# Sliding-window attention and a gated convolution FFN on one core: a written-out order of all instructions replaced by another

## The chip, the cores and the metric

The kernel runs on one NeuronCore of one Trainium2 chip. The time is the device time of one launch in microseconds (us). Engines are named as in the profile: PE (TensorE: matmuls), PEld (its weight loads), DVE (VectorE), ACT (ScalarE), POOL (GpSimd) and SP (SyncE, which here only issues transfers). Each engine carries out its own instructions strictly in the order in which they stand in its program; an instruction that waits holds up everything behind it on that engine.

## The reference

```python
batch, n_heads, seq, head_dim = (8, 8, 576, 64)
...
    scores = scale * np.matmul(q, k.transpose(0, 1, 3, 2))   # scale = 1 / sqrt(64)
    mask = np.abs(pos[:, None] - pos[None, :]) <= 32
    scores = np.where(mask, scores, -1000000000.0)
    attn = softmax(scores)
    x = np.matmul(attn, v)          # heads side by side: (8, 576, 512)
...
    h = np.maximum(x @ w_in, 0.0)   # w_in: 512 x 1024
    for k in range(3):
        conv_out += conv_w[k][None, None, :] * hp[:, k:k + S, :]   # along the sequence, per channel
    gate = 1.0 / (1.0 + np.exp(-conv_out))
    return (h * gate @ w_out)       # w_out: 1024 x 512
```

All inputs and the output are float32.

## The kernel before

**Tiling.** Attention is done in 36 units of two 64-row query tiles each (units 4 and 6 are cut into two halves, a and b); a tile needs 128 keys. The FFN is done in 12 chunks of 384 rows, three chunks to two batches. Products run in bf16 into eight PSUM banks.

**Operations.** `build` lists some 1,200 named operations with the slots that they read and write. The names, which the plan below uses too, are: LQK (load a q or k tile; in `LQKb.yz` b is the batch, y is 0 for q and 1 for k, z the half or 01 pair of heads), CQK (cast it to bf16), TR (transpose it on PE: 18 matmuls), EV (copy the transpose out of PSUM), LV, CV, VO (load v, cast it, copy it shifted by half a tile), LWI, CWI, LWO, CWO (load and cast the two weights), SC (scores), EX (exp, ACT), MA (mask, DVE), AV (attention times v, 16 matmuls), NO (normalize, two DVE instructions), XT and XE (transpose of the result on PE, and its copy out) or, from unit 20 on, XD (the same by a transposing transfer), PH and RE (first FFN product and relu), RO (rotation of h by 32, 64 or 96 partitions, two transfers on SP or two copies on DVE), CO (convolution: 48 small matmuls on diagonal weights), TA (tanh, ACT), GA (gate, DVE), YY (second FFN product: 8 matmuls), YC (copy out of PSUM), YS (store). MK and DG make masks and diagonals. F512 is a matmul of zeros whose result nobody reads.

**What sets the order.** There is no scheduler at build time: `PLAN` is a text of words, carried out from the first to the last (lines 761 to 776). A word is an operation, `/A`, `/D` or `/S` names the engine of a copy or rotation (ACT, DVE, SP), and the digits behind `@` name its PSUM banks. So the text sets the order on every engine and who does each copy. The numbers in `build` (an engine's cost, `size` for a transfer) are not used when the kernel is built; they belong to the search that wrote the text.

**Queues.** All loads, stores, rotations and transposing transfers are issued by SP in the order of the text, except half of each first-batch q or k load, which ACT issues (line 449). q, k and the two weights pass through six staging tiles `st0` to `st5`, so a load waits for the cast of what was there before; v passes through `vst`, with five places. The first-batch loads use st0 to st3; w_in's pieces 1, 2, 3 and 0 use st4, st5, st0 and st1; the four tiles of batch 1 use st2, st3, st4 and st5.

**Lines.** Loads of q and k L450 (batches 0 and 1) and L453, v L461, w_in L475, w_out L487 and L489, store L738, rotation L688 and L689, transposing transfer L651. Copies and casts are L380 on ACT and L382 on DVE; exp L544, mask L615, normalize L634 and L635, relu L682, tanh L715, gate L722; matmuls L390, transposes L393.

Of the kernel before, what the change touches and what calls it, by code (L numbers as in the profile page):

```python
# [72 lines left out]
def build(k, ud=UD):  # L73
# [22 lines left out]
    def load_qk(b, parts):  # L96
        early = b < HB
        for z in parts:
            for y in range(2):
                s, q = nxt("st", NST), nxt("qkb", NQB)  # L100
                add(f"LQK{b}.{y}{z}", {"SP": 1.27 if early else 0.52}, lambda e, a=(b, y, z, s): k.load_qk(*a),
                    w=[("st", s)], size=1.95, desc=256, cnt=2 if early else 1)
                add(f"CQK{b}.{y}{z}", {"DVE": 0.67, "ACT": 1.02},
                    lambda e, a=(s, q): k.cast_qk(e, *a), r=[("st", s)], w=[("qkb", q)], port=1)
                ps = [Slot(), Slot()]
                add(f"TR{b}.{y}{z}", {"PE": 0.27}, lambda e, a=(q, ps): k.turn(*a), r=[("qkb", q)], w=ps, alloc=ps, mode="r64")
                for x in range(2):
                    add(f"EV{b}.{y}{z}{x}", {"ACT": 0.53, "DVE": 0.67}, lambda e, a=(b, y, z, x, ps[x]): k.evac_qk(e, *a),
                        r=[ps[x]], w=[("qkT", b % 2, y, z, x)], uses=[ps[x]])
# [139 lines left out]
F512@0 F512@0 F512@0 F512@0 F512@0 F512@0 F512@0 F512@0 F512@0 F512@0 F512@0 AV0@57 MA1 SC4b@24 NO0.0 EX4b.1 EX4b.0
VO0.11 CWI3/A VO0.02 NO0.1 F512@0 F512@0 AV1@25 MA4b SC5@41 NO1.0 CV0.3/A VO0.13 CWI1/A NO1.1 VO0.12 EX5.1 VO0.03  # L250
LQK1.01 CWI2/D F512@0 F512@0 F512@0 F512@0 AV2@52 XT1@7 NO2.0 AV3@16 XE1/A XT0@3 LQK1.11 NO3.1 SC6a@50 XE0/A NO2.1
AV4a@76 EX5.0 NO3.0 PH0.5a@3 LV1.3 EX6a.1 XT2@4 EX6a.0 NO4a.1 XT3@1 LV1.1 XE2/A CWI0/D LV1.2 RE0.5a XE3/A CV1.0/D
F512@2 F512@2 PH0.1a@3 MA6a LV1.4 CQK1.01/A AV4b@46 NO4a.0 PH0.0a@1 NO4b.0 PH0.7b@5 XT4a@7 NO4b.1 RE0.7b PH0.0b@0
RE0.0a PH0.6b@4 XE4a/D TR1.01@16 CQK1.11/D PH0.7a@7 EV1.010/A EV1.011/D TR1.11@52 LQK2.10 RE0.6b RE0.7a PH1.4a@1
LWO0 EV1.111/D EV1.110/A PH1.0a@7 RE0.0b PH0.4a@6 RE1.0a SC7@25 RE1.4a CV1.1/D RE0.4a SC8@70 CV1.3/D EX7.0 PH0.6a@1
MA5 SC6b@64 EX8.0 PH0.2a@2 CV1.2/D EX6b.0 PH1.3a@7 RE0.1a EX7.1 VO1.00 PH0.5b@6 PH0.3a@3 EX6b.1 CV1.4/D XT4b@5
RE0.2a RE1.3a PH0.4b@4 RE0.6a VO1.10 PH0.1b@2 RE0.5b EX8.1 RO0.3 PH0.2b@1 MA7 PH0.3b@6 RE0.2b AV5@70 XE4b/A MA6b
LQK2.00 RE0.3a NO5.1 RE0.3b AV6a@15 CQK2.10/A NO5.0 RO0.1 AV6b@36 PH1.5a@0 NO6a.1 XT5@7 RE0.4b NO6a.0 RE1.5a LWO3
PH1.6a@5 NO6b.0 RE1.6a XT6a@1 RE0.1b AV7@04 MA8 XE5/A LWO2 PH1.2a@3 XE6a/A NO7.1 PH1.1a@2 AV8@75 NO6b.1 RE1.1a LWO1
PH1.5b@4 RE1.2a NO8.1 CO0.0@2136 RE1.5b NO8.0 XT6b@4 NO7.0 TA0.03 PH1.2b@5 TA0.00 PH1.7b@7 XE6b/D RE1.2b PH1.3b@0  # L260
GA0.03 TA0.01 PH1.6b@4 RE1.3b PH1.4b@5 RE1.7b GA0.01 TA0.02 RO1.1 XT8@0 XT7@7 GA0.00 RE1.4b PH1.7a@1 RE1.6b XE8/D
XE7/A CO0.1@6524 RO1.2/D CWO3/A PH2.5@7 RO0.2/D TA0.11 PH2.7@0 RE1.7a TA0.13 GA0.11 RO1.3 TA0.12 PH2.6@1 GA0.02
TA0.10 GA0.13 PH2.2@5 RE2.6 CWO0/D RE2.7 TR2.10@43 GA0.12 RE2.2 PH1.0b@1 LQK2.01 GA0.10 PH2.4@0 RE1.0b LV2.3 RE2.5
CWO1/D PH1.1b@1 CO1.0@6257 CWO2/D RE1.1b LQK2.11 EV2.101/D LV2.1 YY0.1@1 TA1.02 EV2.100/D LV2.4 TA1.03 TA1.01 LV2.2
GA1.02 RE2.4 GA1.01 TA1.00 CO1.1@0543 YC0.1/A CQK2.01/D YY0.2@2 TA1.10 GA1.03 TA1.11 GA1.00 CQK2.00/A LV2.0 GA1.10
LQK3.00 GA1.11 TR2.01@67 TA1.12 LQK3.10 TR2.00@01 RO2.2/D EV2.011/A YY0.0@5 LQK3.11 EV2.000/A CQK2.11/D RO2.3 TA1.13
YC0.2/D EV2.001/A TR2.11@07 EV2.010/A GA1.13 PH2.3@1 EV2.110/D EV2.111/A LQK3.01 YC0.0/A PH2.1@6 GA1.12 CV2.4/A
CV2.1/D SC12@07 CV2.3/D SC10@45 EX12.1 YY1.1@3 CV2.2/D LV3.3 EX10.1 VO2.10 RE2.1 CV2.0/D EX10.0 VO2.00 EX12.0 SC9@65
SC11@47 MA10 EX9.0 YY1.2@2 EX9.1 MA12 EX11.1 CQK3.00/D RE2.3 EX11.0 MA9 AV10@75 RO2.1 AV12@16 NO10.0 YY1.0@4
CQK3.10/A NO10.1 LV3.1 MA11 YC1.2/A YC1.1/A NO12.1 AV9@25 LV3.4 CQK3.11/A NO12.0 TR3.00@70 AV11@63 NO9.1 XT12@1 YS0  # L270
EV3.001/A NO11.1 PH2.0@5 YC1.0/A NO9.0 XE12/A XT10@3 TR3.10@40 NO11.0 LV3.2 EV3.000/A XT9@2 XE10/D XT11@6 RE2.0
EV3.101/D CQK3.01/A LV3.0 CO2.0@5371 XE9/D XE11/D TR3.11@20 EV3.100/D TA2.02 PH3.1@6 YS1 TA2.03 GA2.02 TA2.01
LQK4.11 PH3.4@4 GA2.03 RE3.1 LQK4.00 EV3.110/A GA2.01 PH3.0@7 EV3.111/D RE3.4 CO2.1@3162 TA2.00 RE3.0 GA2.00
TR3.01@04 TA2.10 PH3.5@7 TA2.13 GA2.10 TA2.11 PH3.2@5 EV3.011/D EV3.010/A PH3.6@3 TA2.12 GA2.13 RE3.5 GA2.12 PH3.3@4
RE3.2 GA2.11 CV3.3/A SC14@72 RO3.2/D SC13@56 EX14.1 YY2.0@1 EX13.0 CV3.1/D CV3.4/D EX14.0 CV3.2/D EX13.1 MA14
SC15@75 RE3.3 SC16@62 MA13 EX15.0 YY2.1@0 RO3.1 CV3.0/D EX16.0 VO3.10 EX15.1 LV4.2 VO3.00 YC2.0/A LQK4.10 AV13@56
EX16.1 MA15 PH3.7@1 YC2.1/A NO13.0 RE3.6 SC17@27 NO13.1 RE3.7 AV15@50 EX17.1 MA16 RO3.3 CO3.0@3416 EX17.0 NO15.1
# [532 lines left out]
```

## Time and profile before

| | us |
|---|---|
| median of 3 runs (lowest, highest) | 230.08 (228.53, 230.11) |
| the profiled execution, device time | 229.58 |
| its span, first to last instruction | 227.9 |
| PE, DVE, ACT busy in the span | 203.4, 190.1, 180.2 |

The device time of the profiled execution is 1.68 us more than its span. A busy PE is not PE at its peak: matmuls are pipelined and the profile models their ends. In rows of groups stand the busy time, the mean duration of one in ns and the idle time just before them; a timeline's row gives start, length, engine, line, tiles and, in brackets, the idle time before it and what ended it.

### The profile page before, as it was taken

The page shows a single profiled execution, that of the slowest core. Times are in us where ns is not written, and L with a number is a line of the kernel's source. Part 1 is how long each engine was busy: PE and PEld are TensorE (multiplying, and loading weights), DVE is VectorE, ACT ScalarE, POOL GpSimd, SP SyncE. Part 2 cuts the span into 40 slices and gives each one's busy share as a digit, 9 for nine tenths or more (in the row PEclk, how much of TensorE's full clock was granted, in tenths as well). Part 3 has the DMA queues.
Part 4 walks back from the last instruction along what each step waited for, and adds up shares of the span by engine and source line. Part 5 has one row for each costly group of instructions (what it writes and reads, how often), then busy time and mean ns, then how long its engine had stood idle before and what let it go on. Part 6 is the DMA issues. An engine that isn't in the chain of part 4 may idle for free.

```text
span 227.9 us, 8845 instructions
## 1 busy us (share of the span) xinstructions
PE 203.4 (89%) x3711; PEld 121.1 (53%) x3741; DVE 190.1 (83%) x459; ACT 180.2 (79%) x393; POOL 1.2 (1%) x8
## 2 busy tenths in 40 slices
PE   0279789999999999999999999999999979999990
PEld 0174468776445655655556556554655545545450
DVE  7568999999999999999988999879999599574830
ACT  2278688979999999789899998999849876649710
POOL 2000000000000000000000000000000000000000
PEclk9999999999999999999999999999999999999998
DMA  6999699697999996997996795999977854523253
GB/s 196 308 263 278 197 258 248 170 265 181 304 269 325 283 291 199 230 280 219 370 209 124 236 327 117 128 322 148 391 143 174 203 181 89 176 76 141 74 187 102
DMA packets 67187, 49.45 MB, mean 217 GB/s; under 512 B 48044, under 2 KB 53444, under 8 KB 67140
## 3 DMA queue, kind: packets, MB, share of 16 engines
q1 hardware_dynamic: 66528, 47.62, 78.9%
q10 hardware_dynamic: 612, 1.19, 1.6%
q8 instruction: 31, 0.51, 1.0%
q14 instruction: 16, 0.13, 0.2%
HBM read 32.52 MB, written 9.44 MB: 184 GB/s over the span
## 4 chain that ended last, share of the span: by engine, by line
PE 44%; DVE 24%; DMA 11%; ACT 9%; issue 5%; SPq 4%; DVEq 0%; ACTq 0%
PE ps L390 41%; DMA vst<-in_v_dram 6%; DVE gT L722 5%; DVE xn L635 5%; PE ps L393 3%; DMA st<-in_q_dram 3%; ACT hh L682 3%; DVE attn L615 3%; ACT attn L544 2%; DVE vo L382 2%; DVE qkb L382 2%; ACT ps L715 2%; DVE rec L634 2%; DMA hh<-hh 2%; SPq L461 2%
## 5 line engine op out<-in xcount | busy, mean ns | idle before, releaser
L390 PE MATMUL ps<-xT,w_in_sb 128*128 128x385 bf16 (+3 forms) x448 | 72.3, 305 | 1.1 <-DVE w_in_sb L382 0.3
L390 PE MATMUL ps<-w_out_sb,gT 128*128 128x512 bf16 (+1 forms) x269 | 65.0, 373 | 1.8 <-issue 0.5
L682 ACT ACTIVATE hh<-ps 128x385 bf16<-128x385 f32 (+3 forms) x112 | 48.0, 476 | 10.2 <-PE ps L390 9.8
L722 DVE SCALAR_TENSOR_TENSOR gT<-ps,hh 128x384 bf16<-128x384 f32 x96 | 48.7, 550 | 7.4 <-ACT ps L715 6.4
L390 PEld LDWEIGHTS <-w_in_sb 128*128 128x128 bf16 x448 | 39.4, 98 | 24.0 <-issue 3.3
L715 ACT ACTIVATE ps<-ps 128x384 f32<-128x384 f32 x96 | 42.1, 497 | 6.6 <-PE ps L390 6.1
L544 ACT ACTIVATE attn<-ps 128x512 bf16<-128x512 f32 (+1 forms) x76 | 40.6, 615 | 6.0 <-PE ps L390 4.3
L390 PEld LDWEIGHTS <-gT 128*128 128x128 bf16 x296 | 27.1, 97 | 29.1 <-issue 1.3
L635 DVE TENSOR_TENSOR xn<-ps,rec 128x256 bf16<-128x256 f32 (+1 forms) x76 | 32.2, 424 | 2.6
L380 ACT COPY qkT<-ps 128x576 bf16<-128x576 bf16 x42 | 26.4, 672 | 4.7 <-PE ps L393 4.7
L615 DVE TENSOR_TENSOR attn<-attn,masks 128x1024 bf16<-128x1024 bf16 (+1 forms) x38 | 24.5, 659 | 2.5 <-ACT attn L544 2.2
L393 PE MATMUL ps<-ident,qkb 64*128 64x64 bf16 x576 | 14.3, 199 | 11.0 <-DVE qkb L382 10.4
L380 ACT COPY y<-ps 128x512 f32<-128x512 f32 (+1 forms) x27 | 16.4, 612 | 8.5 <-PE ps L390 8.5
L390 PE MATMUL ps<-hh,diag 32*32 32x384 bf16 x1152 | 20.3, 327 | 0.0
L393 PEld LDWEIGHTS <-qkb 64*128 64x128 bf16 x576 | 11.4, 100 | 16.4 <-DVE qkb L382 11.6
L382 DVE COPY qkT<-ps 128x576 bf16<-128x576 bf16 x22 | 16.3, 751 | 3.0 <-PE ps L393 2.8
L382 DVE CAST qkb<-st 128x1152 bf16<-128x1152 f32 x22 | 16.6, 753 | 2.1 <-DMA st<-in_q_dram 2.0
L390 PEld LDWEIGHTS <-attn 128*64 128x64 bf16 x576 | 12.6, 110 | 10.6 <-issue 5.2
L390 PE MATMUL ps<-ve,attn 128*64 128x65 bf16 x320 | 15.6, 197 | 1.4 <-DVE xn L635 1.0
L390 PEld LDWEIGHTS <-diag 32*32 32x32 bf16 x1152 | 11.8, 88 | 7.8 <-issue 4.2
L390 PEld LDWEIGHTS <-qkT 64*128 64x128 bf16 x576 | 11.1, 99 | 7.5 <-issue 6.0
L390 PE MATMUL ps<-qkT 64*128 64x64 bf16 x576 | 13.5, 196 | 1.7 <-DVE qkb L382 1.3
(57 smaller groups left out, 136.6 us busy)
## 6 DMA issues: line engine op xcount, KB each, us to landing
out_dram<-y SPq DMA_DIRECT2D x11, 768.0 KB, 6.3
st<-in_k_dram SPq DMA_DIRECT2D x12, 576.0 KB, 6.6
st<-in_q_dram SPq DMA_DIRECT2D x12, 576.0 KB, 5.7
vst<-in_v_dram SPq DMA_DIRECT2D x24, 256.0 KB, 6.4
vst<-in_v_dram SPq DMA_DIRECT2D x16, 192.0 KB, 5.9
hh<-hh SPq DMA_DIRECT2D x16, 144.8 KB, 3.0
st<-in_moe_w_in_dram SPq DMA_DIRECT2D x4, 512.0 KB, 7.2
st<-in_k_dram SPq DMA_DIRECT2D x6, 288.0 KB, 5.5
```

The source lines that it names most:

```text
L380: self.do(nc.scalar.copy(out=out, in_=in_))
L382: self.do(nc.vector.tensor_copy(out=out, in_=in_))
L390: self.do(self.nc.tensor.matmul(*a, **kw))
L393: self.do(self.nc.tensor.transpose(out=out, in_=in_, identity=ident))
L461: self.do(self.dq.dma_start(self.vst[s0 - lo:s1 - lo, c], self.v_[b, :, s0:s1, :].rearrange("h p d -> p h d")))
L544: self.do(self.nc.scalar.activation(at[:, lo:hi], self.ps(ps)[:, lo:hi], AF.Exp, bias=0.0, scale=self.scale))
L615: self.do(self.nc.vector.tensor_tensor(out=at, in0=at, in1=m, op=ALU.mult))
L634: self.do(self.nc.vector.reciprocal(rec, po[:, :, 64]))
L635: self.do(self.nc.vector.tensor_tensor(out=self.xn[x][lo:hi, 4 * g:4 * g + 4, :], in0=po[:, :, 0:64], in1=rec[:, :, None].broadcast_to([hi ...
L682: self.do(self.nc.scalar.activation(o, i_, AF.Relu, bias=0.0, scale=0.5))
L715: self.do(self.nc.scalar.activation(z, z, AF.Tanh, bias=0.0, scale=1.0))
L722: self.do(self.nc.vector.scalar_tensor_tensor(out=o, in0=z, scalar=1.0, in1=self.taps(kind, 0, 128, 6 + 2 * j + g if j else g, 1), op0=ALU ...
```

## The change

Three numbers of `build` change: what a first-batch q or k load costs SP (1.27 to 0.65) and how long it takes (`size` 1.95 to 1.65, and 2.1 for batch 1). Since these are not used in building, they change nothing by themselves. What changes the program is `PLAN`, which is replaced from its first line to its last.

```diff
-                add(f"LQK{b}.{y}{z}", {"SP": 1.27 if early else 0.52}, lambda e, a=(b, y, z, s): k.load_qk(*a),
-                    w=[("st", s)], size=1.95, desc=256, cnt=2 if early else 1)
+                add(f"LQK{b}.{y}{z}", {"SP": 0.65 if b == 0 else 1.27 if early else 0.52}, lambda e, a=(b, y, z, s): k.load_qk(*a),
+                    w=[("st", s)], size=1.65 if b == 0 else 2.1 if early else 1.95, desc=256, cnt=2 if early else 1)
...
-LQK0.11 LQK0.01 LQK0.10 LQK0.00 MK CQK0.11/D LV0.1 TR0.11@01 CQK0.01/D EV0.111/A TR0.01@23 LQK1.00 EV0.110/A
...
+LQK0.01 LQK0.10 LQK0.00 LQK0.11 MK LV0.4 CQK0.01/D CQK0.10/D TR0.01@01 LQK1.00 TR0.10@23 EV0.011/D LV0.1 CQK0.00/A
...
```

The operations are the same, but for the matmuls of zeros: 25 before, 20 now. Before, 17 of them stand ahead of the first AV, six between it and the first PH, and two between the first and the second PH. Now 7 stand ahead of the first AV, 12 between it and the first PH, and one behind that.

The engines of copies change: CQK 10 on ACT and 22 on DVE before, 11 and 21 now; EV 42 and 22, now 44 and 20; CV 15 and 25, now 13 and 27; CWO 1 and 3, now 3 and 1; XE 10 and 12, now 12 and 10 (the two that move are half-size); YC 27 and 10, now 25 and 12 (one of the two is half-size); of twelve rotations RO by 64 partitions on DVE one, of chunk 10, goes to SP. Ahead of the first CO there are seven CQK on DVE before and five now.

SP's first loads, before; `st` with its number is the staging tile, `vst` is v, 96x8x64 its first or last tile of a batch.

```order
L450 DMA st3_64<-in_k_dram 128x1x576
L450 DMA st2_63<-in_q_dram 128x1x576
L450 DMA st1_62<-in_k_dram 128x1x576
L450 DMA st0_61<-in_q_dram 128x1x576
L461 DMA vst_67<-in_v_dram 128x8x64
L450 DMA st2_63<-in_q_dram 128x1x576 x2
L450 DMA st3_64<-in_k_dram 128x1x576 x2
L461 DMA vst_67<-in_v_dram 96x8x64
L461 DMA vst_67<-in_v_dram 128x8x64
L461 DMA vst_67<-in_v_dram 96x8x64
L475 DMA st0_61<-in_moe_w_in_dram 128x4x256
L475 DMA st4_65<-in_moe_w_in_dram 128x4x256
```

The same place of SP now, from the third load of batch 0 on:

```order
L450 DMA st0_61<-in_q_dram 128x1x576
L450 DMA st3_64<-in_k_dram 128x1x576
L461 DMA vst_67<-in_v_dram 96x8x64
L450 DMA st2_63<-in_q_dram 128x1x576 x2
L461 DMA vst_67<-in_v_dram 128x8x64 x2
L461 DMA vst_67<-in_v_dram 96x8x64
L450 DMA st3_64<-in_k_dram 128x1x576 x2
L461 DMA vst_67<-in_v_dram 128x8x64
L475 DMA st4_65<-in_moe_w_in_dram 128x4x256
L475 DMA st5_66<-in_moe_w_in_dram 128x4x256
L475 DMA st1_62<-in_moe_w_in_dram 128x4x256
L461 DMA vst_67<-in_v_dram 96x8x64
```

The second tile of batch 1 (st3) now stands behind four of the five v tiles of batch 0; the last v tile comes behind it. The v tile of rows 0 to 95, LV0.0, is the last 96x8x64 row ahead of the weights before, and now the one ahead of that st3 row. The fourth piece of w_in (st0) has gone from the first place among the weights to one not shown here, behind the last two tiles of batch 1 (st4, st5).

ACT a little later, around the casts of the first weights, before (`ve0` a cast v tile, `qkT1` batch 1's transposes, `w_in_sb` the weight):

```order
L380 COPY qkT1_78<-ps7_122 128x4x144
L380 CAST ve0_73<-vst_67 128x8x64
L380 COPY qkT1_78<-ps5_120 128x4x144
L380 CAST ve0_73<-vst_67 128x8x64
L544 ACTIVATE attn0_84<-ps4_119 128x256
L544 ACTIVATE attn0_84<-ps2_117 128x256
L380 CAST w_in_sb_79<-st0_61 128x4x256
L380 CAST ve0_73<-vst_67 128x8x64
L380 CAST w_in_sb_79<-st4_65 128x4x256
```

And now:

```order
L380 CAST ve0_73<-vst_67 128x8x64
L380 CAST qkb0_68<-st3_64 128x2x9x64
L544 ACTIVATE attn2_86<-ps2_117 128x512
L380 COPY qkT1_78<-ps4_119 128x4x144
L380 COPY qkT1_78<-ps1_116 128x4x144
L380 COPY qkT1_78<-ps6_121 128x4x144
L380 CAST w_in_sb_79<-st4_65 128x4x256
L380 COPY qkT1_78<-ps0_115 128x4x144
L380 CAST w_in_sb_79<-st5_66 128x4x256
```

The cast of batch 1's second tile (`qkb0<-st3`) has come to ACT from DVE, and the cast of st5, which frees that tile for batch 1's last load, has come from DVE as well.

DVE where batch 7's v is used, before (`attn` masks, `ve1` cast v, `vo1` shifted v, `rec` and `xn` normalize):

```order
L615 TENSOR_TENSOR attn4_88<-attn4_88,masks_83 128x1024
L615 TENSOR_TENSOR attn3_87<-attn3_87,masks_83 128x1024
L382 CAST ve1_74<-vst_67 128x8x64 x3
L382 COPY vo1_76<-ve1_74 64x2080
L615 TENSOR_TENSOR attn0_84<-attn0_84,masks_83 128x1024
L382 COPY vo1_76<-ve1_74 64x2080
L634 RECIPROCAL rec_103<-ps4_119 128x4
```

And now:

```order
L615 TENSOR_TENSOR attn3_87<-attn3_87,masks_83 128x1024
L382 CAST ve1_74<-vst_67 128x8x64
L615 TENSOR_TENSOR attn4_88<-attn4_88,masks_83 128x1024
L634 RECIPROCAL rec_103<-ps2_117 128x4
L635 TENSOR_TENSOR xn1_90<-ps2_117,rec_103 128x256
L382 CAST ve1_74<-vst_67 128x8x64
L382 COPY vo1_76<-ve1_74 64x2080
L615 TENSOR_TENSOR attn0_84<-attn0_84,masks_83 128x1024
L382 COPY vo1_76<-ve1_74 64x2080
```

One of the three casts of v in a row has gone to ACT, and a normalize (two instructions) has come in ahead of the rest. On SP the four late v tiles of batch 7 stood one ahead of chunk 6's store and three behind it; now all four stand behind it. On PE one more PH (four matmuls) now stands ahead of the AV that reads the last `vo1`.

More of the change, by code (lines that the diff above doesn't have):

```diff
@@ L249 @@
[L249 to L253, printed above, removed]
```

151 lines of the change are left out of this document (78 added, 73 removed).

## The prediction

> **What bounds the kernel now.** I read the busy times first, then the span cut into stages, then the chain of waits, and the timelines where the chain points.
>
> ```profile
> PE 203.4 (89%) x3711; PEld 121.1 (53%) x3741; DVE 190.1 (83%) x459; ACT 180.2 (79%) x393; POOL 1.2 (1%) x8
> 20.00:48.00 28.00, 25.18 (x447) 17.57 (x447) 25.76 (x73) 21.31 (x54) 0.00 (x0) 1.00 0.89 232
> 48.00:90.00 42.00, 41.13 (x782) 24.30 (x786) 40.48 (x92) 40.84 (x88) 0.00 (x0) 1.00 0.98 264
> 90.00:190.00 100.00, 96.43 (x1901) 55.97 (x1918) 90.69 (x215) 88.10 (x188) 0.00 (x0) 1.00 0.87 221
> 190.00:223.00 33.00, 32.44 (x406) 16.95 (x408) 19.69 (x44) 19.83 (x47) 0.00 (x0) 1.00 0.42 130
> PE 44%; DVE 24%; DMA 11%; ACT 9%; issue 5%; SPq 4%; DVEq 0%; ACTq 0%
> ```
>
> In a stage's row stand its length, then the busy time of PE, PEld, DVE, ACT and POOL. There are four regimes. From 20 to 48 us DVE is busy 25.76 of 28 and ACT only 21.31, so DVE carries the stage and ACT has 6.7 us free. From 48 to 90 all three are full: ACT has 1.2 us free, DVE 1.5. From 90 to 190 they share the load, with 9.3 us free on DVE and 11.9 on ACT. From 190 on attention is over, DVE and ACT are idle two fifths of the time, and PE alone sets the pace. So a shorter start, or less DVE work while DVE carries, is worth its full size only if the last stage then begins earlier; and no stage has an engine with much to spare.
>
> The two places where the chain of waits runs through a transfer (start, length, what):
>
> ```profile
> 12.84 8.17 DMA vst<-in_v_dram
> 21.04 0.63 ACT ve L380
> 21.69 0.29 DVE vo L382
> ...
> 22.00 0.69 DVE attn L615
> ...
> 176.32 6.18 DMA vst<-in_v_dram
> ```
>
> At the start the last early v tile, LV0.0, is issued at 12.84 and cast at 21.04; the shifted copy and the mask of unit 0 follow, and only then AV0. At 176 the same happens to batch 7's last v tile.
>
> ```profile
> 18.92 2.32 PE L390 MATMUL ps<-zz 128*128 128x512 bf16 x5
> 21.02 2.31 PE L390 MATMUL ps<-zz 128*128 128x512 bf16 x9
> 23.48 0.22 PE L390 MATMUL ps<-ve,attn 128*64 128x65 bf16 x1
> 30.51 0.26 PE L390 MATMUL ps<-xT,w_in_sb 128*128 128x193 bf16 x1
> 48.23 0.47 ACT L715 ACTIVATE ps<-ps 128x384 f32<-128x384 f32 x1 [0.59 <-PE ps L390]
> ```
>
> PE fills the wait with matmuls of zeros; AV0 comes at 23.48, the first PH at 30.51, the first tanh, so the end of the first CO, at 48.23.
>
> **Copies that change engine.** Durations come from the groups of instructions (busy time, then mean ns of one).
>
> ```profile
> L382 DVE CAST qkb<-st 128x1152 bf16<-128x1152 f32 x22 | 16.6, 753 | 2.1 <-DMA st<-in_q_dram 2.0
> L380 ACT CAST qkb<-st 128x1152 bf16<-128x1152 f32 x10 | 12.2, 1216 | 0.0
> L382 DVE COPY qkT<-ps 128x576 bf16<-128x576 bf16 x22 | 16.3, 751 | 3.0 <-PE ps L393 2.8 <-PE ps L390 0.2
> L380 ACT COPY qkT<-ps 128x576 bf16<-128x576 bf16 x42 | 26.4, 672 | 4.7 <-PE ps L393 4.7
> L382 DVE CAST w_out_sb<-st 128x1024 bf16<-128x1024 f32 x3 | 2.0, 683 | 0.0
> L380 ACT CAST w_out_sb<-st 128x1024 bf16<-128x1024 f32 x1 | 1.1, 1088 | 0.0
> L382 DVE CAST ve<-vst 128x512 bf16<-128x512 f32 x25 | 10.2, 424 | 1.9 <-DMA vst<-in_v_dram 1.8
> L380 ACT CAST ve<-vst 128x512 bf16<-128x512 f32 x15 | 10.0, 670 | 2.1 <-DMA vst<-in_v_dram 2.1
> L382 DVE COPY y<-ps 128x512 f32<-128x512 f32 x10 | 6.9, 687 | 2.6 <-PE ps L390 2.4
> L380 ACT COPY y<-ps 128x512 f32<-128x512 f32 x25 | 15.6, 632 | 7.7 <-PE ps L390 7.7
> L382 DVE COPY xT<-ps 128x256 bf16<-128x256 bf16 x2 | 0.6, 286 | 0.0
> L380 ACT COPY xT<-ps 128x256 bf16<-128x256 bf16 x2 | 0.8, 386 | 0.0
> ```
>
> Up to CO9.1, about where the last stage begins, DVE loses two CWO, one CQK, two EV and two half-size XE and gains one YC and two CV: -1.37 - 0.75 - 1.50 - 0.57 + 0.69 + 0.85 = -2.65 us. ACT gets the reverse: +2.18 + 1.22 + 1.34 + 0.77 - 0.63 - 1.34 = +3.54.
>
> Where this lies decides what it is worth. Ahead of the first CO, DVE has two CQK and one half XE less, 1.51 + 0.29 = 1.8 us; one of these casts comes back behind it. ACT has one CQK and one CWO more there, 2.3, in a stage in which it has 6.7 free. So these 1.8 us come off the engine that carries the stage, and I take **-1.8**; at best nothing more of this, at worst 0, if DVE waits that much longer.
>
> Between the first CO and CO9.1 the rest is left: DVE -2.65 + 1.8 = -0.9, ACT +3.54 - 2.3, some +1.2. The two are near each other in free time there, so I take **0**, with -0.9 and +1.2 as ends.
>
> **The loads of the start.** LV0.0 now has batch 1's second tile (two rows of 288 KB) behind it instead of ahead.
>
> ```profile
> 10.00:20.00 10.00, 6.86 (x150) 5.28 (x152) 7.66 (x13) 7.39 (x15) 0.00 (x0) 1.00 1.04 255
> 16.84 0.76 DVE L382 COPY qkT<-ps 128x576 bf16<-128x576 bf16 x1 [1.66 <-PE ps L393]
> ```
>
> At the 255 GB/s of this stage 576 KB are 2.3 us, so LV0.0 lands at about 18.7; the mask of unit 0 (0.69) now stands ahead of the shifted copy and is done by then. AV0 comes at about 18.7 + 0.63 + 0.29, near 19.6 in place of 23.48. But then the next load is late: DVE's cast CV0.2 needs the last v tile, LV0.2, which now has the same tiles ahead of it that LV0.0 had, and one v tile of 256 KB (1.0 us) more, so it lands near 22. The two masks, normalizes and AVs behind that cast wait for it, in order. DVE's old wait of 1.66 for a transpose goes, since that copy is ACT's now; a wait of 1 to 2.5 us for LV0.2 takes its place. I count **0**. The ends are -2.4 (of AV0's lead of 3.9 the 1.5 that the new wait surely takes is gone) and +1.
>
> **The matmuls of zeros.** Five fewer. They stand where PE waits anyway, and cost nothing as long as what follows is not ready. The rows above show what they do: the first five start 0.42 us apart ((2.32 - 0.63) / 4, with 0.63 the last one's length, an estimate), the next nine 0.24, most of them 0.215. So PE runs at half its pace until about 21.3 us, 2.4 us into the row of them. Now seven stand ahead of AV0, and the twelve behind it are cut up by waits. I count 0, since the 18 transposes, AV0 and three more of them follow closely.
>
> [...]
>
> **Batch 7's v tiles.**
>
> ```profile
> 173.78 0.54 SPq L738 DMA_DIRECT2D out_dram<-y  x1
> 174.36 5.50 SPq L461 DMA_DIRECT2D vst<-in_v_dram  x3
> 182.23 0.43 DVE L382 CAST ve<-vst 128x512 bf16<-128x512 f32 x1 [0.94 <-DMA vst<-in_v_dram]
> 184.90 0.22 PE L390 MATMUL ps<-vo,attn 128*64 128x65 bf16 x1 [1.48 <-DVE vo L382]
> ```
>
> PE stands 1.48 us because the last shifted copy of v is late. Now one more PH, four matmuls or some 0.7 us of PE, stands ahead of that AV, and one cast fewer (0.42) ahead of the copy on DVE. Against it, the first of the four tiles now also goes behind chunk 6's store (768 KB). I take **-0.5**, between -1.48 and +1.
>
> **The tail.**
>
> ```profile
> 214.31 8.39 PE L390 MATMUL ps<-w_out_sb,gT 128*128 128x512 bf16 x46
> 214.48 2.42 DVE L722 SCALAR_TENSOR_TENSOR gT<-ps,hh 128x384 bf16<-128x384 f32 x5
> ```
>
> The last gate ends at 216.90; the last chunk's YY begins after the two YY of chunk 10, two fifths of this run (16 of 40 full matmuls' worth), at 217.7. So there is 0.8 us to spare. Now the last chunk's two PH for the rotation by 96 partitions are followed by one other PH and not three, so its rotation starts nearer to the end by two PH, some 1.4 us, which the spare time covers in part. I take **+0.3**, between 0 and +0.6. That one rotation of chunk 10 leaves DVE for SP saves nothing where DVE is idle.
>
> **The sum.** -1.8 + 0 + 0 - 0.5 + 0.3 = -2.0 us. The profiled execution took 229.58 (span 227.9 and 1.68 around it), which gives 227.6; the median of the runs is 0.5 higher, 230.08, which gives 228.1. I forecast between them, 227.8.
>
> **The rivals.**
>
> *The lead is lost* (chance 0.28). The start is earlier, but the full stage from 48 to 90 us takes it back, because ACT, with 1.2 us free there, now has the EV and the CWO that DVE gave up. For it: three engines near full. Against it: 6.7 us of free ACT ahead of it. The time is 230.08 - 0.5 + 0.3 and up to +1.2 for ACT: 229.9 to 231.1.
>
> *SP waits on ACT, and the time rises* (chance 0.17).
>
> ```profile
> 27.32 1.19 SPq L450 DMA_DIRECT2D st<-in_q_dram  x2
> 29.07 1.18 SPq L450 DMA_DIRECT2D st<-in_k_dram  x2
> 30.31 4.56 SPq L461 DMA_DIRECT2D vst<-in_v_dram  x4
> ```
>
> Before, batch 1's last tile was issued at 29.07, right after DVE had cast st5, and batch 1's v from 30.31 on. Now the cast of st5 is ACT's, behind the late tile of batch 1 (1.22), an exp, four copies and another weight; and a fourth w_in piece (512 KB, 2.1 us at 255 GB/s) and part of w_out stand ahead of later loads. If that cast ends 1 us later than before, batch 1's v is 1 + 2.1 us late, and the masks, casts and PH of chunk 0 behind it wait: +3.1, so 233.2. It decides from the point at which SP issues that tile later than 29.07. Against it: the piece of w_in in st5 is the second behind LV0.2, so it lands two pieces (4.1 us) after 22, at about 26, and its cast ends near 27.
>
> *The clock stays low* (chance 0.07). If the twelve pieces between AV0 and the first PH run at 0.42 in place of 0.215, they hold PE 2.5 us longer and take back the gain of 2.0: 230.6.
>
> That the new text does nothing can be ruled out: it sets every engine's order.
>
> **How the numbers follow.** The forecast has 0.48. Its own range is 225.4 (the -2.4 of the loads) to 229.5. The range of 225.2 to 232.0 leaves out the worst half of the second rival and the cases in which loads and batch 7 both go best. About 1% (2.3 us) is what a measurement can tell from no change here. 227.8 is 1.0% below the median, so the forecast's case is split: 0.40 faster by over 1%, 0.08 within. With the first and third rival, and a small part of the second, within 1% has 0.44, slower 0.16.
>
> **What would show it.** Right: AV0 at 19 to 20.5 us, a wait of DVE for v of 1 to 2.5 behind it, the first tanh at 45.5 to 47, DVE busy 187 and ACT 183.5 in the span, PE's wait near 183 under 1 us, and the last stage as long as before. Wrong: batch 1's last tile issued after 29 us, starts of zeros 0.42 apart behind 24 us, ACT without a gap from 45 to 90 and the first tanh's lead gone by then, or a wait of the last YY for a gate of over 1 us.

## The result and the profile after

The changed kernel takes 232.57 us (median of 20 runs, 230.11 to 235.51), the kernel before 229.24 (20 runs, 227.17 to 231.59): a ratio of 1.0139, interval [1.0112, 1.0166]. The medians count all runs; the ratio and its interval, like all that follow, leave out runs over 1.5% above the fastest of the same kernel, among them the profiled runs of `new_to_148`, `late_cv` and `new_again` below. The changed kernel is slower by 1.4%, some 3.2 us, and outside the forecast range of 225.2 to 232.0. The span of its profiled execution is 230.6 us, 2.7 more than before.

The busy times, four stages, and the shares of the chain, of the kernel after:

```profile
PE 202.3 (88%) x3705; PEld 121.0 (52%) x3736; DVE 187.6 (81%) x454; ACT 183.1 (79%) x396; POOL 1.2 (1%) x8
20.00:48.00 28.00, 23.79 (x454) 17.96 (x456) 24.76 (x71) 23.82 (x61) 0.00 (x0) 1.00 0.87 233
48.00:90.00 42.00, 41.20 (x830) 24.55 (x833) 39.42 (x88) 41.05 (x90) 0.00 (x0) 1.00 0.96 267
90.00:190.00 100.00, 93.60 (x1775) 53.72 (x1770) 87.39 (x207) 85.44 (x178) 0.00 (x0) 1.00 0.83 212
190.00:223.00 33.00, 32.03 (x470) 16.57 (x475) 20.65 (x48) 21.44 (x50) 0.00 (x0) 1.00 0.43 112
PE 42%; DVE 16%; DMA 16%; ACT 14%; issue 6%; SPq 5%; DVEq 0%; ACTq 0%
```

DVE and ACT do the amounts of work that were forecast. But from 90 to 190 us PE, DVE and ACT are each 2.7 to 3.3 us less busy than before: all three wait more. DVE's share of the chain fell from 24% to 16%, and transfers rose from 11% to 16%.

The start, on PE and ACT:

```profile
16.16 2.35 PE L390 MATMUL ps<-zz 128*128 128x512 bf16 x6
18.65 0.19 PE L390 MATMUL ps<-ve,attn 128*64 128x65 bf16 x1
46.17 0.88 ACT L715 ACTIVATE ps<-ps 128x384 f32<-128x384 f32 x2
```

AV0 comes at 18.65 (before 23.48), the first tanh at 46.17 (before 48.23; by one and the same tanh, TA0.00, 48.62, so 2.45 us earlier). The lead is lost later. Three stretches there, before and then after:

```profile
142.00:150.00 8.00, 7.90 (x135) 4.54 (x137) 6.50 (x13) 7.44 (x18) 0.00 (x0) 1.00 0.95 163
180.00:186.00 6.00, 4.30 (x93) 2.49 (x92) 4.22 (x11) 4.84 (x11) 0.00 (x0) 1.00 0.65 203
186.00:196.00 10.00, 9.95 (x158) 5.54 (x159) 8.51 (x25) 6.84 (x16) 0.00 (x0) 1.00 0.54 142
```

```profile
142.00:150.00 8.00, 5.98 (x109) 3.28 (x107) 6.06 (x12) 5.51 (x13) 0.00 (x0) 1.00 0.73 173
180.00:186.00 6.00, 5.87 (x87) 3.12 (x79) 4.01 (x9) 4.59 (x10) 0.00 (x0) 1.00 0.98 261
186.00:196.00 10.00, 8.02 (x187) 4.58 (x187) 7.98 (x23) 7.79 (x17) 0.00 (x0) 1.00 0.52 103
```

PE works 1.92 us less in the first and 1.93 less in the last. Of the latter 1.57 is no loss: from 180 to 186 PE works that much more than before, since the kernel before has its own wait for batch 7's v there, from 183.4 on. The chain of waits of the kernel after (start, length, what) names what was waited for:

```profile
143.74 3.65 DMA hh<-hh
147.49 0.57 DVE gT L722
148.09 0.45 PE ps L393 x18
...
153.47 4.54 DMA vst<-in_v_dram
158.03 0.78 DVE ve L382 x2
...
177.77 3.39 SPq L461
181.21 5.14 DMA vst<-in_v_dram
186.37 0.63 ACT ve L380
187.02 0.70 DVE vo L382
187.77 2.81 PE ps L390 x44
```

The first is a rotation of chunk 6, the second a v tile of batch 6, the third batch 7's last v tile, which SP issued only at 181.21, since the tile ahead of it had held SP for 3.39 us. The waits themselves, from DVE's and PE's timelines, and then chunk 6's first gates on DVE in the kernel before:

```profile
147.49 1.02 DVE L722 SCALAR_TENSOR_TENSOR gT<-ps,hh 128x384 bf16<-128x384 f32 x2 [1.24 <-DMA hh<-hh]
148.09 0.59 PE L393 MATMUL ps<-ident,qkb 64*128 64x64 bf16 x29 [1.44 <-DVE gT L722]
187.77 0.22 PE L390 MATMUL ps<-vo,attn 128*64 128x65 bf16 x1 [1.28 <-DVE vo L382]
```

```profile
142.65 0.56 DVE L722 SCALAR_TENSOR_TENSOR gT<-ps,hh 128x384 bf16<-128x384 f32 x1 [0.46 <-ACT ps L715]
144.13 1.02 DVE L722 SCALAR_TENSOR_TENSOR gT<-ps,hh 128x384 bf16<-128x384 f32 x2 [0.26 <-ACT ps L715]
```

SP's own timeline shows why the rotation is late, before and then after:

```profile
134.51 0.54 SPq L688 DMA_DIRECT2D hh<-hh  x1
135.09 1.61 SPq L689 DMA_DIRECT2D hh<-hh  x1
137.42 4.64 SPq L651 DMA_TRANSPOSE xT<-xn  x3
142.15 0.54 SPq L688 DMA_DIRECT2D hh<-hh  x1
```

```profile
136.19 1.36 SPq L651 DMA_TRANSPOSE xT<-xn  x1
137.65 0.54 SPq L688 DMA_DIRECT2D hh<-hh  x1
138.24 0.58 SPq L689 DMA_DIRECT2D hh<-hh  x1
138.91 4.14 SPq L651 DMA_TRANSPOSE xT<-xn  x2
143.15 0.54 SPq L688 DMA_DIRECT2D hh<-hh  x1
```

One of the three transposing transfers now stands ahead of chunk 6's first rotation: it starts at 136.19 and holds SP for 1.36 us. So that rotation is issued at 137.65, 3.1 us later than before. The second rotation stands behind all three in both orders; it is the one in the chain, and is issued 1.0 us later than before (143.15 against 142.15), although chunk 6's first tanh came 1.25 us earlier (140.82 against 142.07).

### The profile page after: what moved, and what is told of

Its sections match the earlier page's. It is cut to its first block, busy times and chain, and to the rows that moved or that the text cites. A ratio compares the mean times of both kernels' runs of the same rounds, so it can differ in the third digit from the quotient of the medians.

```text
span 230.6 us, 8855 instructions
## 1 busy us (share of the span) xinstructions
PE 202.3 (88%) x3705; PEld 121.0 (52%) x3736; DVE 187.6 (81%) x454; ACT 183.1 (79%) x396; POOL 1.2 (1%) x8
## 4 chain that ended last, share of the span: by engine, by line
PE 42%; DVE 16%; DMA 16%; ACT 14%; issue 6%; SPq 5%; DVEq 0%; ACTq 0%
PE ps L390 39%; DMA hh<-hh 5%; DMA st<-in_k_dram 5%; DMA vst<-in_v_dram 4%; DVE gT L722 4%; ACT hh L682 3%; PE ps L393 3%; ACT ps L715 2%; DVE xn L635 2%; ACT attn L544 2%; ACT qkT L380 2%; SPq L461 2%; DVE qkb L382 2%; DVE vo L382 2%; DMA xT<-xn 2%
## 5 line engine op out<-in xcount | busy, mean ns | idle before, releaser
L722 DVE SCALAR_TENSOR_TENSOR gT<-ps,hh 128x384 bf16<-128x384 f32 x96 | 49.4, 551 | 9.7 <-ACT ps L715 5.5
L715 ACT ACTIVATE ps<-ps 128x384 f32<-128x384 f32 x96 | 43.1, 498 | 5.3 <-PE ps L390 5.2
L380 ACT COPY qkT<-ps 128x576 bf16<-128x576 bf16 x44 | 27.2, 660 | 4.0 <-PE ps L393 3.9
L380 ACT COPY y<-ps 128x512 f32<-128x512 f32 (+1 forms) x25 | 14.9, 605 | 10.5 <-PE ps L390 10.5
L382 DVE CAST qkb<-st 128x1152 bf16<-128x1152 f32 x21 | 15.7, 753 | 4.1 <-DMA st<-in_k_dram 2.3
L634 DVE RECIPROCAL rec<-ps 128x4 f32<-128x4 f32 (+1 forms) x76 | 13.3, 175 | 6.0 <-PE ps L390 4.2
L380 ACT CAST qkb<-st 128x1152 bf16<-128x1152 f32 x11 | 13.1, 1195 | 5.7 <-DMA st<-in_q_dram 5.7
L390 PE MATMUL ps<-qkT 64*128 64x64 bf16 x576 | 14.9, 196 | 1.9 <-DVE qkT L382 0.8
```

What stands on the lines that cost most here:

```text
L380: self.do(nc.scalar.copy(out=out, in_=in_))
L382: self.do(nc.vector.tensor_copy(out=out, in_=in_))
L390: self.do(self.nc.tensor.matmul(*a, **kw))
L634: self.do(self.nc.vector.reciprocal(rec, po[:, :, 64]))
L715: self.do(self.nc.scalar.activation(z, z, AF.Tanh, bias=0.0, scale=1.0))
L722: self.do(self.nc.vector.scalar_tensor_tensor(out=o, in0=z, scalar=1.0, in1=self.taps(kind, 0, 128, 6 + 2 * j + g if j else g, 1), op0=ALU ...
```

## The experiments

In what follows, an order such as `new_to_148` has the words of the new text up to the point that stands near 148 us and the remaining operations in the order of the old text, with bank digits changed where two uses would meet:

```diff
-PLAN = old
+PLAN = new[:n] + [w for w in old if w not in new[:n]]
```

**Start or rest (`new_start`, `new_rest`).** The new order up to the second CO of chunk 2, near 80 us, with the old rest, and the reverse. The two theories: the lead of the start is worth its size if the rest is the old one, or it is taken back whatever follows.

> The new order up to the second conv of chunk 2 (where both orders have carried out the same operations), the order before from there on. Theory 1 (the start wins about 2.4 us, as the first tanh at 46.17 in place of 48.62 shows, and the loss lies in the new order of the rest): faster than before by 1.5 to 2.7 us, ratio 0.988 to 0.994, first tanh of chunk 2 still 2.4 us or more early, and the wait of PE for the shifted copy of batch 7's v at about 182 with some 1.5 us as before. Theory 2 (a lead of the start is taken back by whatever follows, since three engines are near full): within 0.4% of before.

> The mirror image: the order before up to the second conv of chunk 2, the new order from there on. Theory 1: slower than before by what the change lost (1.4%, 3.2 us) and by the 2.4 us of the start that are missing here, together 5 to 6 us, ratio 1.021 to 1.026. Theory 2: as slow as the new order, ratio 1.012 to 1.016.

Measured: `new_start` 229.27 us, 1.0001 [0.9971, 1.003]; `new_rest` 232.29, 1.0104 [1.0039, 1.0169]. So the new start gains nothing, and the new rest carries the loss. Theory 1 is wrong about the start: in `new_start` the first tanh of chunk 2 came at 78.00, 0.4 us later than in the profile of before, and not 2.4 earlier. `new_rest` is below what either theory expected, though its interval covers the second.

**One place at a time (`v7_first`, `rot6_first`).**

```diff
-YS6 ... LV7.1 ... LV7.3 ... LV7.2 ... LV7.4
+LV7.1 LV7.3 LV7.2 LV7.4 YS6
```

```diff
-XD24 ... RO6.3 ... XD23 ... XD22 ... RO6.1
+RO6.3 XD24 ... RO6.1 XD23 ... XD22
```

> The new order, with the four late v tiles of batch 7 issued ahead of chunk 6's store, nothing else moved. Theory 3 (that store fills the queue, so that the third v tile takes 3.39 us to issue and the fourth is issued at 181.21, 4.9 us later than before): the fourth is issued by 178, PE's wait of 1.28 us for the last shifted copy goes, and the time falls by 1.0 to 2.0 us, ratio to before 1.005 to 1.010. Rival (the tiles are late because SP is late already at the rotations, 166.43 in place of 164.62): the time falls by less than 0.6 us.

> The new order, with the two rotations of chunk 6 on SP (96 partitions, then 32) issued ahead of the transposing transfers of units 24, 23 and 22. Theory 4 (the gates of chunk 6 stand 1.4 and 1.2 us for these rotations, which land at 142.6 and 147.4, and PE's 2.1 us of lost work between 140 and 150 come from that): the gates' waits fall under 0.4 us each, the lead of 2 us at 141 is kept to 150, and the time falls by 1.0 to 2.0 us, ratio to before 1.005 to 1.010. Rival (the transfers of units 22 to 24, now later, hold up chunk 7's first product by as much): the time stays within 0.6 us.

`v7_first`: 231.10, 1.0115 [1.0068, 1.0163]. The mechanism of theory 3 came true, its gain did not: against 1.0139 the time fell by 0.5 us, which is within the noise and what the rival expected. The timelines show the wait gone: the last shifted copy of v starts at 184.32 in place of 187.02, right behind the mask.

```profile
183.59 0.69 DVE L615 TENSOR_TENSOR attn<-attn,masks 128x1024 bf16<-128x1024 bf16 x1
184.32 0.69 DVE L382 COPY vo<-ve 64x2080 bf16<-64x2080 bf16 x1
```

`rot6_first`: 232.33, 1.0169 [1.0117, 1.0221]: no gain from this alone. In its profile DVE's gates no longer wait for the rotations, but PE waits 0.95 us for a transposing transfer at 145.4, as the rival says.

**Where the loss begins (`new_to_120`, `new_to_148`, `new_to_175`), and the old order with its v tiles first (`old_v7`).**

> The new order up to the second normalize of unit 20 (about 120 us), the order before from there on. Theory A (most of the loss arises where gates wait for late rotations, 140 to 150 us): the old order carries those rotations in time, so the time is that of the kernel before, ratio 0.997 to 1.003. Theory B (batch 7's late v tiles alone): the same, 0.997 to 1.003. Theory C (the new order loses a little everywhere): 1.003 to 1.006. If the lead of the start lived on to here and were kept: 0.994.

> The new order up to the tile of chunk 6's first unit of tanh (about 148 us), the order before from there on. Theory A: the gates of chunk 6 still wait, so 1.5 to 2.2 us of the loss are here, ratio 1.006 to 1.010. Theory B: 0.998 to 1.003. Theory C: 1.006 to 1.009, with no stretch of the trace that loses over 1 us.

> The new order up to just ahead of chunk 6's store and batch 7's v tiles (about 175 us), the order before from there on, so one v tile and the store are issued as before. Theory A: the loss is there in full but for that of the v tiles, ratio 1.008 to 1.012. Theory B: no loss, 0.998 to 1.004, and the last shifted copy of v begins less than 1 us later than before. Theory C: 1.010 to 1.013.

> The kernel before, with three of batch 7's v tiles issued ahead of chunk 6's store instead of behind it; nothing else differs. If the store of 768 KB is what delays them: the last v tile lands 1 to 2.5 us earlier, PE's wait of 1.5 us near 183 goes, and the time falls by up to 1 us, ratio 0.995 to 0.999. If they wait for buffers or the transfers' own width instead, nothing moves: 0.998 to 1.002.

Measured: 1.0067 [1.0005, 1.0128], 1.0136 [1.0061, 1.0211] and 1.0251 [1.0192, 1.0309]; `old_v7` 1.0006 [0.9936, 1.0076]. None of the theories fits: the time rises with the cut, and the last exceeds the whole new order. The place where one order is joined to the other can cost time of its own (in `new_to_175` PE waits 3.03 us at 175.4, longer than anywhere behind the start in the other runs), so these three don't place the loss. But their traces showed what nobody had asked: `new_to_148` lost 3.6 us near 52, where the same words had cost `after` nothing.

**PE's instructions.** In those traces PE stops within a group of 18 transpositions, and nothing that the profile shows ends the wait. First the group in the kernel after, then in a second execution of the same kernel, `new_again`, which was run with this in its expectation (the two theories of which it speaks are S and T of the next part):

```profile
50.96 0.44 PE L393 MATMUL ps<-ident,qkb 64*128 64x64 bf16 x18
```

```profile
51.60 0.43 PE L393 MATMUL ps<-ident,qkb 64*128 64x64 bf16 x17
54.44 0.19 PE L393 MATMUL ps<-ident,qkb 64*128 64x64 bf16 x1 [2.40 <-issue]
```

> The changed kernel once more, for a profile of a second execution and for its ratio on the chip of this comparison. Both theories: 1.011 to 1.017. If PE's instruction fetch is what takes the lead at 51 to 55 us: its packet ends 1.3 to 1.5 us ahead of the transposition that follows when PE waits there, and 1.8 us or more ahead of it when PE does not.

The page of each run has a DMA queue of its own for this; here that of the kernel after (packets, MB, share of 16 engines):

```profile
q8 instruction: 31, 0.51, 1.1%
```

These are 31 packets of 16 KB. By the trace's records of packets (us; "first tanh" is TA0.00; "packet" is when the packet was under way; "lag" is from its end to the 18th transposition; "TA" is the time between two fixed tanh around that). The last four rows have the old order here: "18th" is there the matmul at the same count of PE's instructions, and "TA" is between two other tanh.

```
run          first tanh  packet        18th    lag   PE waits  TA
after          46.17     47.79-49.11   51.20   2.09   0        4.15
new_third      46.15     47.81-49.16   51.18   2.02   0        4.15
v7_first       46.11     47.75-49.09   51.15   2.06   0        4.15
rot6_first     46.57     48.16-49.50   51.61   2.10   0        4.15
new_to_175     45.88     47.87-49.07   50.93   1.85   0        4.16
start_v7       46.57     48.26-49.64   51.61   1.97   0        4.15
new_to_120     46.90     50.41-51.38   52.76   1.38   0.63     4.89
mid_fix        49.46     52.84-53.95   55.24   1.29   0.85     5.11
new_start      46.23     49.31-51.49   52.82   1.34   1.37     5.63
late_fix       46.27     50.48-51.59   53.10   1.51   1.61     5.87
late_cv        46.75     51.28-52.39   53.69   1.30   1.72     7.65
new_to_148     46.66     51.18-52.45   53.87   1.42   1.85     7.73
new_again      47.15     51.97-53.07   54.44   1.37   2.40     8.33
before         48.62     51.42-52.82   54.23   1.41   0        3.50
old_again      47.28     49.81-51.21   53.04   1.83   0        3.51
old_v7         46.80     48.97-50.25   52.56   2.31   0        3.50
new_rest       48.51     50.42-51.71   54.12   2.40   0        3.50
```

Where PE waits, the transposition comes 1.29 to 1.51 us behind the packet, in seven of seven; where the new order does not wait, 1.85 to 2.10, and nowhere in the table less than 1.29. So I take this as a wait for PE's own instructions, whose packets the page counts among those of the same 16 DMA engines as the loads. That the queue carries PE's instructions is inferred from this and from the page's counts: 31 packets beside 7,441 instructions of PE and PEld, 240 to a packet, while DVE has 454 and ACT 396. The same instructions can wait 0 or 2.4 us. In the four executions with the old order PE never waited here, though the instruction at the same count came only 1.41 us behind its packet in one. No packet of the table was under way earlier than 190 instructions ahead of the transposition.

The last column shows a step. Waits up to 1.61 us cost about what they last (5.87 - 4.15 = 1.72). From 1.72 us on they cost 1.75 us more (7.65 - 4.15 - 1.72 = 1.78; 1.73 and 1.78 in the next two). The stages of `new_again` show why; in each row the last but two is the granted clock:

```profile
50.00:54.00 4.00, 2.04 (x78) 1.54 (x76) 3.87 (x9) 3.14 (x8) 0.00 (x0) 1.00 1.02 310
54.00:58.00 4.00, 3.56 (x14) 1.73 (x14) 1.61 (x4) 1.93 (x3) 0.00 (x0) 0.66 0.86 218
```

After the wait the clock falls to half, by the trace's records for 3.4 us. The same followed PE's wait of 3.03 us in `new_to_175` and, for 6.8 us, one of 1.77 near 41 in `mid_fix`. No fixed length decides it: in `late_light` (below) waits of 0.74 and 0.70 us at 41.3 and 42.8 were followed by a fall, in `start_shift` 1.05 and 0.70 at the same place were not.

**SP's row mended at all three places (`mid_fix`, `late_fix`).** `mid_fix` has the rotations as above and one v tile of batch 6 earlier; `late_fix` has batch 7's v tiles ahead of the store too. Only SP's order changes.

```diff
-XD24 ... RO6.3 ... XD23 ... XD22 ... RO6.1 ... YS4 ... RO7.3 ... LV6.2
+RO6.3 XD24 ... RO6.1 XD23 ... XD22 ... LV6.2 YS4 ... RO7.3
```

> The new order with three steps of SyncE earlier and nothing else changed: chunk 6's rotations by 96 and by 32 partitions each ahead of the transposing transfer that they stood behind, and batch 6's v tile 2 ahead of chunk 4's store. If the stretch from 140 to 165 us is lost to what stands in SyncE's row (theory S): gate GA6.01 within 0.5 us of its time in the new order less the 1.4 us that PE waits there, the cast of that v tile near 150 in place of 158 us, 1.5 to 2.3 us of the 3.3 us back, ratio 1.003 to 1.007. If the transfers themselves set the pace there (theory T): the waits move to other transfers, ratio 1.010 to 1.016.

> As the kernel with three steps earlier, and batch 7's four v tiles ahead of chunk 6's store too, so that all three places at which the new order lost PE work have SyncE's row mended. Theory S: the whole loss goes and the earlier start shows, ratio 0.992 to 1.001. Theory T: 1.008 to 1.014, as with the v tiles alone (1.0115).

Measured: `mid_fix` 232.60, 1.0112 [1.0072, 1.0151]; `late_fix` 229.44, 1.0034 [0.9999, 1.0069]; `new_again` on the same chip 233.83, 1.0196 [1.0133, 1.0259]. Theory S is right about most of the loss: seven words moved on SP take it from 1.4% (2.0% on this chip) to 0.3%. Which of them count is not shown: added to the other three the v tiles bring 0.8% or 1.8 us (1.0112 to 1.0034), alone no more than the noise (`v7_first`). Theory S is wrong on the tile of batch 6: its cast comes at 160.1 and 158.5 us, against 158.0 in the kernel after, since it stands there in DVE's row. And the mended place at 142 us is not free of waits. In `late_fix` PE waits for a transposing transfer there, which now stands behind the rotations:

```profile
146.63 2.15 PE L390 MATMUL ps<-xT,w_in_sb 128*128 128x386 bf16 x12 [1.10 <-DMA xT<-xn]
142.00:150.00 8.00, 6.85 (x173) 3.82 (x143) 6.72 (x14) 6.76 (x15) 0.00 (x0) 1.00 0.68 191
```

That is the part in which theory T is right: of the 1.92 us of PE's work, 0.87 came back. How much of this is due to the words one profile cannot tell, since a third execution of the unchanged new order (`new_third`, below) was busy for 7.69 us in this window.

**The best of both (`start_v7`), a lighter start, a moved fetch, earlier casts.** `start_v7` is `new_start` with three v tiles of batch 7 ahead of the store; its new part, too, reaches to near 80 us, and not to 48 as its expectation says. `start_light` and `late_light` issue two loads of batch 2 later; `start_shift` cuts the matmuls of zeros:

```diff
-LQK2.01 ... LQK2.00 ... RO1.1 ... RO1.3 ... CQK2.01 ... CQK2.00 ... GA1.00 ... GA1.10
+RO1.1 ... RO1.3 LQK2.01 LQK2.00 ... GA1.00 CQK2.01 ... GA1.10 CQK2.00
```

```diff
-        self.mm(self.banks[at][:, 0:n], self.zz[:, 0:128], self.zz[:, 0:n], start=True, stop=True)
+        for j in range(0, n, 128):
+            self.mm(self.banks[at][:, j:j + 128], self.zz[:, 0:128], self.zz[:, 0:128], start=True, stop=True)
```

```diff
-LV6.2 ... LV6.1 ... NO26.1 ... YC6.1 ... CV6.2 ... CV6.1
+LV6.1 LV6.2 ... CV6.2 NO26.1 ... CV6.1 YC6.1
```

The last of these diffs is `late_cv`, on top of `late_fix`.

> The new order up to about 48 us, the order before from there on, and three of batch 7's v tiles ahead of chunk 6's store: a kernel that has the earlier start and neither of the late losses. If the start's lead lives (less what PE's instruction fetch takes at 51 to 55 us, 0 to 3.6 us): ratio 0.992 to 0.998. If it is lost for good: 0.998 to 1.002.

> The kernel start_v7 with two loads of 576 KB (batch 2) issued behind chunk 1's two rotations by 32 and 96 instead of 5 us earlier, and their casts each a few gates later; nothing else. If the burst of loads delays PE's instruction packet (theory F): the packet that comes near 48 to 52 us ends by 50 us, PE does not wait at the 18th transposition near 52, and the time is 0.5 to 1.3 us below start_v7's, ratio 0.992 to 0.998. If something else takes the start's lead: 0.998 to 1.003, or more where the later loads make the casts wait.

> The kernel late_fix (new order, SyncE's row mended at three places) with the same two loads later. Theory F: no wait at the 18th transposition and no fall of the clock behind it, ratio 0.995 to 1.001 against late_fix's 1.0034; if the fetch plays no part: 1.002 to 1.006.

> The kernel start_v7 with every matmul of zeros cut into four of a quarter of the columns, which adds some 120 to 160 instructions to PE's stream ahead of 30 us and no work. Theory F: the boundary of fetched instructions then lies that many instructions earlier, so PE never waits at the 18th transposition near 52 us; if it waits, it is some 2 us of work earlier, 1.3 to 1.4 us behind the end of a packet. If the wait belongs to the transposition itself: it stays there in about half of the executions. Time: 0.994 to 1.003 either way.

> The kernel late_fix with batch 6's v tile 1 loaded earlier and the casts of its v tiles 1 and 2 on VectorE ahead of the normalizes and chunk 7's gates instead of behind them. If these late casts are what holds 140 to 165 us: VO6.00 begins 2 us or more earlier relative to what stands ahead of it, PE work lost between 140 and 165 us falls from 1.1 to 1.4 us to under 0.5, ratio 0.998 to 1.002. If not: 1.002 to 1.006.

Measured: `start_v7` 228.67, 0.9992 [0.9956, 1.0028]; `start_light` 1.0084 [1.0055, 1.0113]; `late_light` 1.0103 [1.0058, 1.0148]; `start_shift` 1.0132 [1.0087, 1.0178]; `late_cv` 1.0069 [1.0024, 1.0113].

None of them is measurably faster than the kernel before, and the last four are slower by 0.7 to 1.3%. In neither of the light kernels did PE wait at the 18th transposition, but their packets ended only 1.30 and 1.46 us ahead of it, so they came just in time rather than early. Two executions do not show that the burst of loads is what delays the packet. The loads themselves came too late: `start_light` is 0.7 us ahead of `start_v7` at the end of chunk 1's tanh and 1.1 behind it at the first of chunk 2. In `start_shift` there was no wait at the 18th transposition either, but its one profile cannot tell that from chance; PE waited 1.49 us for a transposing transfer near 176 instead, and why its median is 1.4% above that of `start_v7` stays open. `late_cv` speaks against the casts as the cause: they came 4.5 and 1.3 us earlier, and as much was lost between 140 and 165 us as in `late_fix` (PE busy 23.38 and 23.36 of 25 us).

The record also shows why `start_v7` and `old_v7` gain so little from batch 7's v tiles. In the old order they trade one wait for another: the store that now stands behind the tiles frees its source tile later, ACT waits for that, and PE waits for ACT. In `old_v7` (start, length, and the wait in brackets):

```profile
180.88 0.59 ACT L380 COPY y<-ps 128x512 f32<-128x512 f32 x1 [1.62 <-DMA out_dram<-y]
181.91 0.64 PE L390 MATMUL ps<-qkT 64*128 64x64 bf16 x32 [1.46 <-ACT hh L682]
```

These 1.46 us take the place of the kernel before's 1.48; in `start_v7` the same wait is 1.32.

**Two more executions of the two kernels as they are.**

> The kernel before, once more, for a profile of another execution. If the start belongs to the order: first tanh between 46.8 and 48.7 us, and PE does not wait for its instruction packet near 52 to 54 us. If the old order can be hit by the fetch as well: a wait of PE of over 0.5 us there that ends 1.3 to 1.4 us behind the packet.

> The changed kernel a third time, for a profile of another execution: first tanh between 45.9 and 47.2 us, PE's wait at the 18th transposition near 52 us in about one of two executions, and PE's waits of over 0.8 us at 145 to 148 and at 186 to 190 us in each, as in the first two profiles of it (in the second, the first of the two was shorter).

`old_again` took 228.68 us and began the first tanh at 47.28, without a wait for instructions. `new_third` took 229.94; the expectation of its waits was wrong: PE was busy for 7.69 of 8 us between 142 and 150, and its wait for batch 7's v, 0.81 us, was the shortest of the three. So these waits, too, vary from one execution to the next; the medians, not one profile, say what they cost.

Two tanh serve to compare executions piece by piece, since both texts have the same PE work ahead of them but for the matmuls of zeros: the first of chunk 2 and the first of chunk 6 (us; from one mark to the next):

```
run          to chunk 2   to chunk 6   to the end
before         77.60        64.47        85.78
old_again      76.30        64.32        86.33
after          76.51        64.31        89.76
new_third      76.47        64.56        87.06
new_again      81.28        64.93        87.98
v7_first       76.44        64.42        86.87
mid_fix        80.43        64.16        87.00
late_fix       78.29        64.39        86.77
```

Between chunks 2 and 6 all eight agree within 0.8 us, so nothing is lost there. The new order loses behind chunk 6's first tanh, 87.1 to 89.8 us against 85.8 and 86.3, on average 2.2. With SP's row mended at one place, two or three it takes 86.8 to 87.0, so single executions do not tell these three apart.

## Why the prediction was wrong, by its own steps

- **Copies that change engine, -1.8 at the start.** The size was too large, and that the copies bring the lead is not shown, since no run moves them alone. The two first profiles show -2.45, but the old order began the first tanh at 46.80 to 48.62 in four executions (mean 47.80), the new one at 45.88 to 49.46 in thirteen (mean 46.68): -1.1. The profile of before was a late one, and a lead read from one profile on each side holds that chance. Nor is the first tanh a fair mark: the new text has AV8 behind the first CO, the old one ahead of it. At the first tanh of chunk 2 the six executions of the new order that never waited for instructions stand at 76.2 to 76.9 us (mean 76.6), the four of the old at 76.3 to 77.9 (mean 77.1). At the first tanh these six had led by 1.6 (mean 46.2). So 0.5 is what is left of the 1.8 forecast, without any wait for instructions.
- **What takes this lead was in no step.** At 51 to 55 us the new order waits for PE's instructions in seven of thirteen executions, 10.4 us in all, and the clock's fall adds 1.75 in three of them. Even the ten others wait 4.5 us, or 0.45 each, as much as the lead at chunk 2. That fits `new_start`, which gained nothing, but the sum rests on few executions and is not proved. PE's instruction packets were in the page that I read, as 1% of a queue, and I passed over them.
- **Between the first CO and CO9.1, 0 (-0.9 to +1.2).** This step failed. It weighed DVE against ACT and counted 0, while the loss is of SP: which of its transfers stands behind which. With seven words of SP's row moved, and nothing else, the ratio falls from 1.0139 (1.0196 on that chip) to 1.0034. The place is behind chunk 6's first tanh, where the new order takes 2.2 us more on average; in the first profile 142 to 150 us alone lost 1.92 us of PE. I looked at SP's row at the start and at batch 7, and not in between, though the whole text was new.
- **Batch 7's v tiles, -0.5 (-1.48 to +1).** The gain did not come. PE's wait there did get shorter, 1.28, 1.12 and 0.81 us in three executions against 1.48 and 1.56, but behind it, near 195, the new order waits another 0.60 to 0.65 for a transposing transfer, which the old one does not: 1.93, 1.72 and 1.42 in all. I named the store ahead of the first tile as something against the gain, and gave it no price. That the last shifted copy began 2.87 us later than before says little, since chunk 8's first tanh was late by 2.4 (171.03 against 168.60) already. Moving the tiles ahead of the store was worth 1.8 us by the ratios on top of `mid_fix`, and nothing measurable alone or in the old order.
- **The loads and zeros of the start, 0 each.** Right on the place, and better than feared: AV0 at 18.65 against some 19.6, and the wait for LV0.2 did not come. The first zeros start 0.40 to 0.43 us apart and last 0.61 to 0.63 each; from 18.13 us to the last recorded at 28.96 they last 0.38 to 0.39, and where two or three stand together they start 0.22 apart.
- **The tail, +0.3.** It cost nothing: from the first PH of chunk 10 to the last copy it takes 30.7 us in both.
- **The rivals.** "SP waits on ACT" had the time nearest to this, 233.2, by chance: its mechanism is refuted, since batch 1's last tile was issued at 25.2 us, not behind 29.07. "The lead is lost" (229.9 to 231.1) names something that happened, but not its mechanism: with 0.95 us of ACT free, the stage from 48 to 90 gives PE 41.20 us of work against 41.13. "The clock stays low" is refuted at its place, since no zeros start 0.42 us apart behind 17.84 us; that pieces cut up by waits would stay slow was an estimate of mine, which no run shows. The clock fell at another place.
- **The range.** The upper ends of the steps (0, +1.2, +1, +1 and +0.6) add up to 3.8 us above the time before, 233.9, which covers the result. The range of 225.2 to 232.0 did not carry these ends.

What stays open: which transfers delay PE's packet, which of the seven words count, and what is left of the loss of `late_fix` (0.3%, its interval touches 0). In its profile PE still waits 2.0 us for transposing transfers from chunk 2 on, against at most 0.2 in three profiles of the old order. Not shown either is why the new order is hit at 52 us and the old one was not in four executions.

## What to carry to other kernels

When a new order is judged, the row of the engine that only issues transfers deserves the same reading as those that compute: for each transfer, what now stands ahead of it, and who waits. A lead should be read at a mark ahead of which both orders have done the same work: 1.6 us at the first tanh were 0.5 at chunk 2, in executions that had not waited in between for instructions. And a difference of 1 to 2 us between two profiles needs a second profile of each. Words can be moved back one at a time: seven words moved in SP's row recovered most of what a whole new order had lost.

## What the runs showed of the hardware

- ACT's 284 exps, relus and tanhs began in the order of the text, by kind, in the profiles of before and after, and so did the 174 and 166 groups into which PE's matmuls and transpositions fall by kind.
- The instruction queue that I take for PE's had 31 packets of 16 KB, which the page counts among those of the DMA engines. The same packet was under way 4 us later in one execution than in another (51.97 against 47.79), and PE waited 2.40 us in the midst of a group of transpositions. The DMA engines were full in both (a share of 1.05 and 1.06 from 46 to 50 us), so fullness alone does not explain it.
- Behind the start, each of five waits of PE of 1.72 us and more was followed by 3.4 us at half clock (6.8 in one), which cost some 1.75 us on top in the three where it was measured. No single wait up to 1.61 was, but two of 0.74 and 0.70 close together were once.
- Executions of the same program differ by up to 1.8 us at the first tanh (46.80 to 48.62 for the same words); the difference is there by VectorE's cast of an early v tile (CV0.2, 21.24 to 23.03 us), and was still there at the first tanh of chunk 2 (76.39 and 77.60).
